# A linear-attention and token/channel mixer kernel: a corrected and searched plan, products of zeros ahead of the first work, transposes moved from TensorE to transfers

## The chip, the cores and the metric

The kernel runs on one NeuronCore of a Trainium2 chip. The core has five engines that run their own queues in order and meet at semaphores: TensorE (PE in the profile; its weight loads are shown apart as PEld), VectorE (DVE), ScalarE (ACT), GpSimd (POOL) and SyncE (SP), which here only issues transfers. The metric is the device time of one execution in microseconds.

## The reference, cut to what matters

Inputs: q, k, v, f_logit of shape (4 batches, 8 heads, 768 steps, 48), and four weight matrices. The output is (4, 768, 384).

```
f = 1 / (1 + exp(-f_logit))
for t in range(768):
    state = f[:, :, t, :, None] * state + outer(k[:, :, t], v[:, :, t])
    y[:, :, t] = q[:, :, t] @ state
x = y, heads side by side                       # (4, 768, 384)
h = relu(x.T @ w_tok1) @ w_tok2                 # 768 -> 256 -> 768 over the steps
u = x + h.T
out = u + relu(u @ w_ch1) @ w_ch2               # 384 -> 1536 -> 384 over the channels
```

## The kernel before, in words

**Attention.** The 768 steps of a batch are cut into 6 chunks of 128. For a chunk, ScalarE makes the log of the gates (exp, ln and a bf16 copy, `gates`, lines 324 to 326) and VectorE or GpSimd the rounding rest (329, 332). TensorE sums the logs along the chunk (`sums`, 350 to 353; the 128 x 1 products of 350 and 351 give the chunk's whole sum). ScalarE takes the exponentials `G`, `Gi` and `glast` (361, 363, 366). VectorE scales q and k to `qh` and `kh` (369, 371). TensorE turns both, four 128 x 128 blocks each (`turn`, 382), VectorE copies the eight blocks from PSUM to `qkT` (386). `scores` (396) are eight products of 48 rows, two at a time in the two halves of the array's rows; VectorE masks them to `AmT` (403). `parts` (419) are eight products kh.T @ v, 64 columns wide, in the two halves of the array's columns; VectorE adds them to the running `state` (426, 429, 431), and ScalarE or GpSimd writes the bf16 copy `state_bd`, head by head on the diagonal (a helper, lines 311 and 315). `outs` makes y from the state of the chunk before (448) and from `AmT` and v (455); two copies bring y to `x_bf` and `x_nat` (helper, 311 and 313).

**Mixer.** For a batch: `tok1` 12 products (480) and two ReLUs to `h1T` (484), `tok2` 12 products (492), `u` = x + h (496), its bf16 copy `u_bf` (311), 18 transposes `ut` (508) with their copies to `uT` (513), `ch1` 24 groups of three products (524) with a ReLU each to `zT` (534 on ScalarE, 536 on VectorE), `ch2` 6 groups of twelve (546) with the last addition (552) and a store from SP (555).

**What sets the order.** Nothing is scheduled at run time. Every step is an `Op` with the engines that may run it, a rank, what it needs and makes, and a cost (`Plan.cost`). `Plan.order` simulates the engines with these costs: again and again it takes the op that can start first, and among equals the one of lower rank. It chooses the engine, and the PSUM bank (8 of them) out of the same simulation. The functions are then called in the order of the planned starts, which gives each engine its queue. The ranks come from `due` and `ranks`.

**Transfers.** f of batch 0 comes chunk by chunk from SP, everything else from GpSimd's queue, which casts fp32 to bf16; `mark` (270) is a small write on GpSimd that holds back an f load of SP. q, k, v and f have three buffers each. SP also issues the 24 stores of the output (192 KB each).

Of the kernel before, what the change touches and what calls it, by code (L numbers as in the profile page):

```python
# [17 lines left out]
NBANK = 8  # L18
RING = 16384

# [19 lines left out]
class Plan:  # L40
# [58 lines left out]
    def order(self):  # L99
        for op in self.ops:  # L100
            first = op.before | ({op.behind} if op.behind else set())
            op.missing = len(first)
            for x in first:
                x.after.append(op)
        free = {e: 0.0 for e in (PE, ACT, DVE, POOL, SP)}
        ready = {e: [] for e in free}
        banks = [0.0] * NBANK
        wire = 0.0
        landed: list = []
        done = []  # L110

        def offer(op):
            t = max([x.end for x in op.before], default=0.0)
            if op.kind[0] == "load" and op.engines == (POOL,) and op.kind[3]:
# [3 lines left out]
                for at, rows in reversed(landed):  # L118
                    held += rows
                    if held > RING:  # L120
                        t = max(t, at)
                        break
            for e in op.engines:
                ready[e].append((t + (WAKE[e] if t else 0.0), op))

        for op in self.ops:
            if not op.missing:
                offer(op)
        while len(done) < len(self.ops):
            best = None  # L130
            for e, line in ready.items():
                for t, op in line:
                    if op.engine is not None:
                        continue
                    t = max(t, free[e])
                    if op.bank is not None and op.bank.at is None:
                        t = max(t, min(banks) + 55)
                    if best is None or (t, op.rank) < best[0]:
                        best = ((t, op.rank), e, op)
            (t, _), e, op = best  # L140
            ready[e] = [(a, o) for a, o in ready[e] if o is not op and o.engine is None]
            if op.bank is not None and op.bank.at is None:
                op.bank.at = min(range(NBANK), key=lambda j: banks[j])
                banks[op.bank.at] = math.inf
            own, till = self.cost(op, e)
            op.engine, op.start = e, t
            free[e] = t + own
            op.end = t + till
            if op.kind[0] == "load":
                size = op.kind[3]  # L150
                if size:
                    wire = max(wire, t + 1700) + size
                    op.end = wire + 1100
                if size and e == POOL:
                    landed.append((op.end, op.kind[2]))
            if op.bank is not None:
                op.bank.users -= 1
                if not op.bank.users:
                    banks[op.bank.at] = op.end
            done.append(op)  # L160
            for x in op.after:
                x.missing -= 1
                if not x.missing:
                    offer(x)
        return sorted(done, key=lambda o: o.start)
# [7 lines left out]
def kernel(  # L173
# [20 lines left out]
    NB = 3  # L194
# [23 lines left out]
    G = [st([128, H, D], BF16, f"G{i}") for i in range(2)]  # L218
    Gi = [st([128, H, D], BF16, f"Gi{i}") for i in range(2)]
    qh = [st([128, H, 64], BF16, f"qh{i}") for i in range(2)]  # L220
    kh = [st([128, H, 64], BF16, f"kh{i}") for i in range(2)]
    qkT = [st([128, 8, 128], BF16, f"qkT{i}") for i in range(2)]
    AmT = [st([128, 8, 128], BF16, f"AmT{i}") for i in range(2)]
    glast = [st([128, HP], FP32, f"glast{i}") for i in range(2)]
    state = st([128, HP, D], FP32, "state")
    tsum = st([128, HP, D], FP32, "tsum")
    state_bd = [st([128, HP, 2 * D], BF16, f"state_bd{i}") for i in range(2)]
# [5 lines left out]
    uT = st([128, 3, S], BF16, "uT")  # L233
# [3 lines left out]
    ones_bf = st([128, 1], BF16, "ones_bf")  # L237
    banks = [ps.tile([128, 512], FP32, tag=f"ps{i}", name=f"ps_{i}") for i in range(NBANK)]
# [7 lines left out]

    def load(what, b, c=None, engine=POOL):
        for n in what:
# [6 lines left out]
            add(engine, 0.0, lambda eng=eng, into=into, of=of: eng.dma_start(out=into, in_=of),  # L255
# [4 lines left out]
    def load_w(name, dst, src, size):  # L260
        add(POOL, 0.0,
# [3 lines left out]
    def once(engine, fn, make, own):  # L265
        add(engine, 0.0, fn, make=make, kind=("fix", own, own))

    def mark(b, c):

        add(POOL, 0.0, lambda: nc.gpsimd.memset(f_sb[b][0:1, 0:1, c, 0:1], 0.0), make=[("f", b, c)],  # L270
# [8 lines left out]
    once(POOL, lambda: make_upper_triangular(nc, tri_bf, val=1.0, diag=True), ["tri"], 550)  # L279
    once(POOL, lambda: make_identity(nc, ident), ["ident"], 550)  # L280
    once(DVE, lambda: nc.vector.memset(ones_bf, 1.0), ["ones"], 60)
    for i in range(2):
        for n, tl in (("L", Lhi[i]), ("L", Llo[i])):
            once(DVE, lambda tl=tl: nc.vector.memset(tl[:, :, :, D:64], 0.0), [("L", i, c) for c in range(NCH)], 400)
        for n, tl in (("qh", qh[i]), ("kh", kh[i])):
            once(DVE, lambda tl=tl: nc.vector.memset(tl[:, :, D:64], 0.0), [(n, i)], 120)
        once(DVE, lambda i=i: nc.vector.memset(state_bd[i], 0.0), [("sbd", i)], 220)
    for c in range(1, NCH):
        load("kq", 0, c)
# [26 lines left out]


# [17 lines left out]
    def attention(b, c, r):  # L335
        i, nb = c % 2, b % NB
# [43 lines left out]
        def turn(src, o):  # L380
            for hp in range(HP):
                nc.tensor.transpose(turned()[:, o + hp, :], blk(src)[:, hp, :], ident)  # L382
# [3 lines left out]
        add(DVE, r, lambda: nc.vector.tensor_copy(qkT[i], turned()), make=[("qkT", i)], bank=p_t,  # L386
            kind=("el", 1024, True, 2))
# [11 lines left out]
        add(PE, r, lambda: None, need=[("qkT", i)], bank=p_a[0], kind=("mm", 1))  # L399
        two = add(PE, r, scores, need=[("qkT", i)], bank=p_a[1], kind=("mm", 270))  # L400
# [9 lines left out]
        if not last:  # L410
            p_d = Bank()

            def dg():
                return banks[p_d.at][:, 0:HP * D].rearrange("p (hp e) -> p hp e", e=D)

            def parts():
                for h in range(H):
                    hp, par = h // 2, h % 2
                    nc.tensor.matmul(dg()[par * 64:par * 64 + 64, hp, :], lhsT=kh[i][:, h, :],  # L419
                                     rhs=v_sb[nb][:, h, c, :], start=True, stop=True)  # L420

            add(PE, r, parts, need=[("kh", i), vk], bank=p_d, kind=("mm", 210))
            gb = glast[i].unsqueeze(2).broadcast_to((128, HP, D))
            small = ("el", HP * D, True, 1)
            if c == 0:
                add(DVE, r, lambda: nc.vector.tensor_tensor(state, dg(), gb, ALU.mult),
                    need=[("glast", i)], make=["state"], bank=p_d, kind=small)
            else:
# [187 lines left out]
```

## Time and profile before

| | |
|---|---|
| median of 3 runs | 189.12 us (188.26 to 189.91) |
| the profiled execution | 188.64 us, of which its span is 186.8 us (1.84 us lie around the span) |
| TensorE busy | 172.5 us, 92% of the span, 1768 products |
| VectorE, ScalarE, GpSimd busy | 129.7, 126.9, 65.9 us |
| first product of TensorE | 6.08 us after the start of the span |
| first `ch1` product of batch 0 | 37.75 us |
| transfers | 19.95 MB; GpSimd's casting loads take 91.9% of the transfer time |

How to read it: a product's duration on TensorE includes its way through the array, and products overlap, so the pace is the distance between starts: a row "x8" of the timeline shows the start of the first and the time until the last has ended. The chain of waits follows what ended last back to the start, end to end, so there the lengths add up to the span. An engine's idle time matters only where something on that chain waits for it.

### The profile page before, as it was taken

How to read it: one execution, taken by the hardware profiler on the slowest of the kernel's cores; microseconds unless marked ns; L12 is line 12 of the kernel's file. 1: busy time of each engine (PE TensorE's matmuls, PEld its weight loads, DVE VectorE, ACT ScalarE, POOL GpSimd, SP SyncE). 2: the span in 40 equal slices, each digit the busy share in tenths (PEclk: the TensorE clock that was granted, in tenths of full speed). 3: DMA queues.
4: the chain of work that ended last, by engine and by line, in shares of the span. 5: the costliest groups of instructions: out<-in, count | busy, mean ns of one | idle time of the engine just before them, and what ended most of it. 6: DMA issues, size and time to landing. Idle time of an engine off the chain costs nothing.

```text
span 186.8 us, 4480 instructions
## 1 busy us (share of the span) xinstructions
PE 172.5 (92%) x1768; PEld 109.6 (59%) x1768; DVE 129.7 (69%) x295; ACT 126.9 (68%) x309; POOL 65.9 (35%) x78
## 2 busy tenths in 40 slices
PE   0589997799999999999999999999999999999992
PEld 0256664366667656676665665766666656656650
DVE  4387985749998999999988758977686638300222
ACT  4779963779983499999999935657875116698000
POOL 7999893275791444504621411011011000000000
PEclk9999999999999999999999999999999999999998
DMA  7999999999999999999992121011000121110222
GB/s 102 140 171 154 156 208 245 186 160 194 143 135 238 174 149 172 242 200 109 83 116 14 52 78 42 0 46 44 4 0 4 55 75 40 46 42 0 81 91 84
DMA packets 88437, 19.95 MB, mean 107 GB/s; under 512 B 81152, under 2 KB 87600, under 8 KB 88416
## 3 DMA queue, kind: packets, MB, share of 16 engines
q0 software_dynamic: 78720, 13.77, 91.9%
q1 hardware_dynamic: 9696, 5.90, 10.8%
q8 instruction: 14, 0.23, 0.5%
q14 instruction: 7, 0.06, 0.1%
HBM read 25.17 MB, written 4.72 MB: 160 GB/s over the span
## 4 chain that ended last, share of the span: by engine, by line
PE 84%; ACT 6%; DVE 3%; issue 2%; DMA 2%; POOL 1%; POOLq 0%; DVEq 0%; ACTq 0%
PE ps L524 26%; PE ps L546 24%; PE ps L382 7%; PE ps L480 5%; PE ps L396 4%; PE ps L492 3%; PE ps L455 3%; PE ps L419 3%; PE ps L352 2%; PE ps L508 2%; PE ps L353 2%; DMA f_sb<-in_f_logit_dram 2%; PE ps L448 2%; ACT u_bf L311 2%; ACT x_bf L311 1%
## 5 line engine op out<-in xcount | busy, mean ns | idle before, releaser
L546 PE MATMUL ps<-w_ch,zT 128*128 128x384 bf16 x288 | 54.1, 327 | 0.0
L524 PE MATMUL ps<-uT,w_ch 128*128 128x384 bf16 x288 | 52.6, 327 | 0.0
L534 ACT ACTIVATE zT<-ps 128x384 bf16<-128x384 f32 x76 | 36.5, 490 | 8.3 <-PE ps L524 7.9
L546 PEld LDWEIGHTS <-zT 128*128 128x128 bf16 x288 | 26.8, 98 | 16.5
L524 PEld LDWEIGHTS <-w_ch 128*128 128x128 bf16 x288 | 26.3, 97 | 15.9
L403 DVE TENSOR_TENSOR AmT<-ps,tri_bf 128x512 bf16<-128x512 f32 x48 | 30.6, 683 | 5.2 <-PE ps L396 5.0
L552 DVE TENSOR_TENSOR x_nat<-x_nat,ps 128x384 f32<-128x384 f32 x24 | 13.2, 550 | 22.9 <-PE ps L546 22.5
L255 POOL DMA_DIRECT2D q_sb<-in_q_dram x14 | 15.4, 1099 | 13.8 <-issue 5.7
L311 ACT ACTIVATE x_bf<-ps 128x384 bf16<-128x384 f32 x20 | 9.9, 494 | 12.9 <-PE ps L455 12.7
L255 POOL DMA_DIRECT2D k_sb<-in_k_dram x14 | 15.5, 1108 | 7.6 <-DMA f_sb<-in_f_logit_dram 4.5
L361 ACT ACTIVATE G<-ps 128x384 bf16<-128x384 f32 x24 | 11.7, 488 | 7.9 <-PE ps L353 7.8
L386 DVE COPY qkT<-ps 128x1024 bf16<-128x1024 bf16 x24 | 16.4, 685 | 0.8 <-PE ps L382 0.7
L255 POOL DMA_DIRECT2D v_sb<-in_v_dram x14 | 15.5, 1104 | 4.1 <-issue 2.5
L496 DVE TENSOR_TENSOR x_nat<-x_nat,ps 128x384 f32<-128x384 f32 x24 | 11.5, 548 | 4.1 <-PE ps L492 4.1
L311 ACT ACTIVATE u_bf<-x_nat 128x384 bf16<-128x384 f32 x24 | 11.4, 523 | 4.1 <-DVE x_nat L496 4.1
L315 POOL CAST state_bd<-state 48x192 bf16<-48x192 f32 x10 | 3.4, 343 | 29.8 <-DVE state L431 24.3
L324 ACT ACTIVATE f_sb<-f_sb 128x384 f32<-128x384 f32 x24 | 12.0, 523 | 2.7 <-DMA f_sb<-in_f_logit_dram 2.6
L480 PE MATMUL ps<-x_bf,w_tok 128*128 128x384 bf16 x48 | 12.3, 340 | 1.0 <-ACT x_bf L311 1.0
L536 DVE TENSOR_SCALAR zT<-ps 128x384 bf16<-128x384 f32 x20 | 10.4, 553 | 3.7 <-PE ps L524 3.6
L311 ACT ACTIVATE state_bd<-state 48x192 bf16<-48x192 f32 x30 | 10.8, 360 | 2.9 <-DVE state L431 2.6
L350 PE MATMUL ps<-ones_bf,Lhi 128*128 128x1 bf16 x80 | 7.0, 167 | 6.1 <-ACT Lhi L326 6.1
L326 ACT ACTIVATE Lhi<-f_sb 128x384 bf16<-128x384 f32 x24 | 12.2, 522 | 0.3
(58 smaller groups left out, 276.3 us busy)
## 6 DMA issues: line engine op xcount, KB each, us to landing
out_dram<-x_nat SPq DMA_DIRECT2D x24, 192.0 KB, 1.9
f_sb<-in_f_logit_dram POOLq DMA_DIRECT2D x3, 1152.0 KB, 11.0
f_sb<-in_f_logit_dram SPq DMA_DIRECT2D x6, 192.0 KB, 4.0
k_sb<-in_k_dram POOLq DMA_DIRECT2D x12, 96.0 KB, 6.3
q_sb<-in_q_dram POOLq DMA_DIRECT2D x12, 96.0 KB, 5.9
v_sb<-in_v_dram POOLq DMA_DIRECT2D x12, 96.0 KB, 6.0
w_ch<-in_moe_w_ch_dram POOLq DMA_DIRECT2D x2, 576.0 KB, 11.0
w_ch<-in_moe_w_ch_dram POOLq DMA_DIRECT2D x1, 1152.0 KB, 14.6
```

The lines of the kernel that those rows point to most:

```text
L255: add(engine, 0.0, lambda eng=eng, into=into, of=of: eng.dma_start(out=into, in_=of), make=[(n, b % NB, j) for j in (range(NCH) if c is No ...
L311: nc.scalar.activation(out_, in_, AF.Copy, bias=0.0, scale=1.0)
L324: add(ACT, r, lambda: nc.scalar.activation(fb, fb, AF.Exp, bias=0.0, scale=-1.0), make=[key], kind=el)
L326: add(ACT, r, lambda: nc.scalar.activation(hi, fb, AF.Copy, bias=0.0, scale=1.0), need=[key], make=[lk], kind=el)
L382: nc.tensor.transpose(turned()[:, o + hp, :], blk(src)[:, hp, :], ident)
L386: add(DVE, r, lambda: nc.vector.tensor_copy(qkT[i], turned()), make=[("qkT", i)], bank=p_t, kind=("el", 1024, True, 2))
L403: add(DVE, r, lambda p=p: nc.vector.tensor_tensor(AmT[i][:, 4 * p:4 * p + 4, :], banks[p_a[p].at].rearrange("s (hp t) -> s hp t", t=C), tb ...
L480: add(PE, rank("tok1", rt), lambda rt=rt, kt=kt, pm=pm: nc.tensor.matmul(banks[pm.at][:, 0:DM], lhsT=w_tok1[:, kt, rt * 128:(rt + 1) * 128 ...
L524: nc.tensor.matmul(banks[pm.at][:, 0:384], lhsT=w[:, kt, c0:c0 + 128], rhs=uT[:, kt, cols], start=(kt == 0), stop=(kt == 2))
L534: nc.scalar.activation(zT[:, cc, cols], banks[pm.at][:, 0:384], AF.Relu, bias=0.0, scale=1.0)
L546: nc.tensor.matmul(banks[pm.at][:, 0:DM], lhsT=zT[:, kt, tt * 128:(tt + 1) * 128], rhs=w_ch2[:, kt, :], start=(kt == 0), stop=(kt == 11))
L552: add(DVE, rank("ch2", tt), lambda un=un, pm=pm: nc.vector.tensor_tensor(un, un, banks[pm.at][:, 0:DM], ALU.add), make=[("x_nat", xn, tt)] ...
```

## The change

In the kernel it does eight things.

1. **The plan's model.** `Plan.order` is replaced by `attempt`, which simulates as before, with some mended costs: a product knows its way through the array ("row" for `scores`, "col" for `parts`, "" for the rest), a change of way takes `TURN` = 105 ns, and a ready product of another way is held back by rank (`HOLD`). Each engine starts at its own `FIRST`.
2. **The search.** `search` draws noise on the ranks, simulates again, and keeps what is no worse: 3000 tries on the part up to batch 0's `uT`, 800 on the whole. The seed is fixed, so the built order is always the same.
3. **Products of zeros.** Until 28.5 us of the plan's time the last PSUM bank is kept from other use, and wherever TensorE's plan has a hole a 128 x 128 product of zeros is put in (`rest`): 135 of them in the built program, 69 of these ahead of the first real product.
4. **Transposes by transfer.** In batches 2 and 3 (`TURNED`) `qh` and `kh`, now one tile `qkh`, are turned by one transposing transfer from SP into `qkT`, 12 in all, in place of 8 TensorE transposes and the VectorE copy. In batch 2 (`TURNED_U`) `u_bf` is turned by two such transfers. `uT` is laid out anew, [128, 6, 3, 128].
5. **Parts by pairs.** In batch 3 (not in `BYHEAD`) `parts` are four full products of 96 columns, of which the diagonal blocks are used, in place of eight narrow ones; the first VectorE step after them goes by halves of the partitions.
6. **Three buffers** in place of two for `G` to `state_bd` (`NI`).
7. **Freer engines.** The copies of y, and the ReLUs to `h1T`, may go to ScalarE or VectorE in every batch; in batch 0 the copy to `qkT` goes in two halves to either. `state_bd` is written by two full-height steps with a 0/1 scale (`own`), in batch 3 by ScalarE or GpSimd.
8. GpSimd makes the triangle and the identity in another order beside its loads.

In the order of the built program, counted: TensorE changes its way through the array 87 times before and 56 times after; from the first `ch1` product on 66 and 34 times. `turn` has 192 transposes before and 96 after, `ut` 72 and 54.

```diff
+TURN = 105
+HOLD = 2000.0
+WARM = 28500
+TRIES = (3000, 800)
+FIRST = {PE: 0.0, ACT: 0.0, DVE: 820.0, POOL: 1250.0, SP: 750.0}
...
+        if what == "turn":
+            return 1230, 2000 + 17 * n[0]
+        if what == "two":
+            return (470, 553) if engine == DVE else (514, 617) if engine == ACT else (700, 700)
...
+        free = dict(FIRST)
+        ready: dict = {e: {} for e in free}
+        banks = [0.0] * (NBANK - 1) + [WARM]
...
+                    if best is None or t <= best[0]:
+                        r = rank[k] + (HOLD if e == PE and self.ops[k].way not in (mode, None) else 0.0)
+                        if best is None or t < best[0] or r < best[1]:
+                            best = (t, r, e, k)
+            t, _, e, k = best
+            op = self.ops[k]
+            if e == PE and op.way is not None:
+                if op.way != mode:
+                    t = max(t, free[PE] + TURN)
+                mode = op.way
...
+            if op.kind[0] == "turn":
+                late = min(max(wire - t - 1000, 0), 2600)
+                wire = max(wire, t + 1500) + 16 * op.kind[1]
+                end[k] = t + till + late
...
+    def search(self, rank, tries, n, worth, rnd):
+        found = self.attempt(rank, n)
+        best, rank = worth(found), list(found[1])
+        for _ in range(tries):
+            far, share = rnd.choice((300, 1000, 3000)), rnd.choice((0.02, 0.1, 0.5))
+            other = [r + (rnd.gauss(0, far) if rnd.random() < share else 0) for r in rank]
+            now = self.attempt(other, n)
+            if worth(now) <= best:
+                best, rank = worth(now), other
+        return rank
...
+        head = self.search(rank[:n], TRIES[0], n, begin, rnd)
+        found = self.attempt(head + rank[n:])
+        rank = self.search(head + found[1][n:], TRIES[1], None, lambda found: found[0], rnd)
...
+        out, t = [], 1600.0
+        for o in sorted(self.ops, key=lambda o: o.start):
+            if o.engine == PE and o.kind[1] > 1:
+                while t < min(o.start, WARM) - 250:
+                    out.append((t, rest))
+                    t += 56 if t > 4500 else 107
+                t = max(t, o.start + self.cost(o, PE)[0])
+            out.append((o.start, o.fn))
...
-    NB = 3
+    NB, NI = 3, 3
+    SPLIT = (0,)
+
+    TURNED_U, TURNED = (2,), (2, 3)
+    BYHEAD = (0, 1, 2)
...
-        add(PE, r, lambda: turn(qh[i], 0), need=["ident", ("qh", i)], bank=p_t, kind=mms(*[C] * 4))
-        add(PE, r, lambda: turn(kh[i], 4), need=["ident", ("kh", i)], bank=p_t, kind=mms(*[C] * 4))
-        add(DVE, r, lambda: nc.vector.tensor_copy(qkT[i], turned()), make=[("qkT", i)], bank=p_t,
-            kind=("el", 1024, True, 2))
+        if b in TURNED:
+            add(SP, r, lambda: nc.sync.dma_start_transpose(qkT[i], qkh[i].rearrange("t n d -> t (n d)")),
+                need=[("qh", i), ("kh", i)], make=[("qkT", i, 0), ("qkT", i, 4)], kind=("turn", 64))
+        else:
+            add(PE, r, lambda: turn(blk(qh[i]), 0), need=["ident", ("qh", i)], bank=p_t, kind=mms(*[C] * 4))
+            add(PE, r, lambda: turn(blk(kh[i]), 4), need=["ident", ("kh", i)], bank=p_t, kind=mms(*[C] * 4))
...
+                dg2 = banks[p_d.at][:, 0:DM].rearrange("p (h e) -> p h e", e=D)
+                for hp in range(HP):
+                    nc.tensor.matmul(dg2[:, 2 * hp:2 * hp + 2, :], lhsT=blk(kh[i])[:, hp, :],
+                                     rhs=v_sb[nb][:, 2 * hp:2 * hp + 2, c, :], start=True, stop=True)
...
+            op = add(ACT if b <= 2 else (ACT, POOL), r, None, need=["own", ("state", 0), ("state", D)], make=[("sbd", i)], kind=("two",))
+
+            def spread(op=op):
+                for par in range(2):
+                    half = state_bd[i][:, :, par * D:par * D + D]
+                    if op.engine == ACT:
+                        nc.scalar.activation(half, state, AF.Copy, bias=0.0, scale=own[:, par:par + 1])
+                    else:
+                        nc.gpsimd.tensor_scalar(half, state, own[:, par:par + 1], None, ALU.mult)
...
-            op = add(ACT if b == 0 else (ACT, DVE), r, None, make=[key], bank=p_y, kind=el)
+            op = add((ACT, DVE), r, None, make=[key], bank=p_y, kind=el)
...
+        if b in TURNED_U:
+            for th in range(2):
+                tts = slice(3 * th, 3 * th + 3)
+                add(SP, rank("ut", 3 * th), lambda tts=tts: nc.sync.dma_start_transpose(
+                    uT[:, tts].rearrange("p tt d t -> p (tt d) t"), u_bf[:, tts, :].rearrange("t tt d -> t (tt d)")),
+                    need=[("u_bf", tt) for tt in range(3 * th, 3 * th + 3)],
+                    make=[("uT", d, tt) for tt in range(3 * th, 3 * th + 3) for d in range(3)], kind=("turn", 72))
...
+    def rest():
+        nc.tensor.matmul(banks[NBANK - 1][:, 0:128], lhsT=nil, rhs=nil, start=True, stop=True)
+
+    nc.vector.memset(nil, 0.0)
+    for fn in plan.order(rest):
+        fn()
```

More of the change, by code (lines that the diff above doesn't have):

```diff
@@ L97, in cost, with attempt, offer @@
         return n[0], n[1]
[L99 to L108, printed above, removed]
+    def attempt(self, rank, n=None):
+        n = n or len(self.ops)
+        missing = [len(o.first) for o in self.ops[:n]]
+        start, end, engine, at = [0.0] * n, [0.0] * n, [None] * n, {}
+        users = {b: b.users for b in self.banks}
+        free = dict(FIRST)
+        ready: dict = {e: {} for e in free}
+        banks = [0.0] * (NBANK - 1) + [WARM]
+        wire, mode = 0.0, ""
         landed: list = []
-        done = []
-        def offer(op):
-            t = max([x.end for x in op.before], default=0.0)
+        left = n
+        def offer(k):
+            op = self.ops[k]
+            t = max([end[x] for x in op.data], default=0.0)
             if op.kind[0] == "load" and op.engines == (POOL,) and op.kind[3]:
@@ L117, in offer @@
                 held = op.kind[2]
-                for at, rows in reversed(landed):
+                for when, rows in reversed(landed):
                     held += rows
                     if held > RING:
-                        t = max(t, at)
+                        t = max(t, when)
                         break
             for e in op.engines:
[L124 to L128, printed above, removed]
@@ L129, in order @@
-        while len(done) < len(self.ops):
-            best = None
-            for e, line in ready.items():
[L132 to L144, printed above, removed]
+                ready[e][k] = t + (WAKE[e] if t else 0.0)
@@ L145, in order @@
             own, till = self.cost(op, e)
-            op.engine, op.start = e, t
+            engine[k], start[k] = e, t
             free[e] = t + own
[L148 to L155, printed above, removed]
+            end[k] = t + till
@@ new lines, in attempt @@
+        return max(end), start, end, engine, at
+    def search(self, rank, tries, n, worth, rnd):
[8 more added lines that the diff above has]
+        return rank
@@ L433, in attention @@
-            for rows, cols in ((slice(0, D), slice(0, D)), (slice(64, 64 + D), slice(D, 2 * D))):
-                op = add(ACT if b <= 2 else POOL, r, None, need=["state"], make=[("sbd", i, cols.start)],
-                         kind=("el", HP * D, False, 1))
-                op.fn = lambda op=op, rows=rows, cols=cols: copy_on(
-                    op.engine, state_bd[i][rows, :, cols], state[rows])
+            whole, halves = (slice(0, 128), None, (0, D)), []
+            for rows, cols in ((slice(0, 64), slice(0, D)), (slice(64, 128), slice(D, 2 * D))):
+                halves.append((rows, cols, (cols.start,)))
```

209 lines of the change are left out of this document (144 added, 65 removed).

## The prediction, made before the changed kernel had run

> **What bounds the kernel now.** I read the page first: busy time, the slices, and the chain that ended last.
>
> ```profile
> PE 172.5 (92%) x1768; PEld 109.6 (59%) x1768; DVE 129.7 (69%) x295; ACT 126.9 (68%) x309; POOL 65.9 (35%) x78
> ...
> PE   0589997799999999999999999999999999999992
> ...
> PE 84%; ACT 6%; DVE 3%; issue 2%; DMA 2%; POOL 1%; POOLq 0%; DVEq 0%; ACTq 0%
> ```
>
> 84% of the chain is TensorE. The digits below 9 lie in the first eight slices (37 us) and the last. Next the waits of TensorE, in total:
>
> ```profile
> PE ps L350 <- ACT Lhi L326: 6.1, 1, 6.1
> PE ps L480 <- ACT x_bf L311: 1.0, 2, 0.6
> PE ps L396 <- DVE qkT L386: 0.8, 1, 0.8
> ```
>
> Apart from the first 6.1 us no wait totals over 1.0 us. Then TensorE's timeline, for its pace.
>
> ```profile
> 26.04 1.06 PE L382 MATMUL ps<-ident,kh 128*128 128x128 bf16 x8
> 26.89 1.17 PE L480 MATMUL ps<-x_bf,w_tok 128*128 128x384 bf16 x3
> ...
> 33.12 2.33 PE L492 MATMUL ps<-h1T,w_tok 128*128 128x384 bf16 x12 [0.41 <-ACT h1T L484]
> ...
> 37.75 6.50 PE L524 MATMUL ps<-uT,w_ch 128*128 128x384 bf16 x39
> ...
> 54.56 0.81 PE L546 MATMUL ps<-w_ch,zT 128*128 128x384 bf16 x4
> 55.30 0.40 PE L396 MATMUL ps<-qkT 48*128 48x128 bf16 x8
> 55.63 0.82 PE L546 MATMUL ps<-w_ch,zT 128*128 128x384 bf16 x4
> ...
> 171.40 11.86 PE L546 MATMUL ps<-w_ch,zT 128*128 128x384 bf16 x72
> ```
>
> Eight transposes take 26.89 - 26.04 = 0.85 us early, 106 ns each; four at 53.15 take 0.23, 56 each. Until 28.5 us every product runs at half pace, though the slices' granted clock reads 9 there. The last 72 products, chain time 11.71 us, give 162 ns for 384 columns. The two groups around 55.30 price a change of the array's way: four products should take 0.65 but the scores start after 0.74. The chain shows both exits:
>
> ```profile
> 46.95 0.24 PE ps L419 x8
> 47.19 0.59 PE ps L524 x3
> ...
> 54.72 0.65 PE ps L546 x4
> 55.37 0.33 PE ps L396 x8
> 55.70 0.76 PE ps L546 x4
> ```
>
> 0.76 against 0.65 for four, 0.59 against 0.49 for three: 0.10 us per change, in or out. Scores cost (0.33 - 0.10)/8 = 29 ns each, parts (0.24 - 0.09)/8 = 19.
>
> **A check by adding up.** From the first ch1 at 37.75 us to the end TensorE has 576 ch and 72 tok products x 162 ns = 105.0; 144 + 54 transposes x 56 = 11.1; sums 36 x 162 and 120 x 25 = 8.8; scores 144 x 29 = 4.2; parts 120 x 19 = 2.3; y 60 x 42.5 and 144 x 25 = 6.2; 66 changes x 0.10 = 6.6. Sum 144.2. The trace has 145.3 (37.75 to 183.1, the last start plus its 0.16), so real stalls are 1.1 us, and 3.7 us follow (the last addition, a store of 1.9, the end). This part is TensorE's queue; before it lies a stretch bound by waits, half pace and loads.
>
> **Part by part.**
>
> *Transfers in place of transposes.* 96 x 56 = 5.4 us for q and k, 18 x 56 = 1.0 for u leave TensorE, all in the dense part. VectorE loses 12 copies of 685 ns and 6 of 348, 10.3 us beside the path. It is needed: VectorE is busy 19.1 and 18.9 of 20 us from 60 to 100 us, and a denser TensorE asks the rest of its work sooner.
>
> The cost is the wait. `scores` now wait for a transfer, and behind them in TensorE's queue stands everything else. In the built order I added up TensorE's work between a chunk's `sums` and its `scores`: batch 2 11.2, 17.8, 16.4, 15.5, 23.3, 27.0 us; batch 3 7.0, 11.5, 10.9, 17.7, 10.0, 7.8. Before, batch 3 had 4.3 to 6.1 and no stall. Of the 4.3, 0.45 + 0.2 went to the transposes and 0.7 to the copy, so exponentials and scaling need at most 2.9. That leaves 4.1 and 4.9 us for the two tightest transfers, 7 or more for the others. For u, 6.25 us lie between the third tok2 and ch1; addition and cast took at most 2.2 before, so 4.05 are left (about 0.4 less where GpSimd casts: its nearest row, L332, has 933 ns against 523). ScalarE's queue loses nothing by that.
>
> No transposing transfer is in the trace. SP's stores bound it: 1.9 us for 192 KB in the median, 7.0 at worst, between 56 and 85 us under the loads. A q, k transfer has 256 KB, so 2.5 at the quiet rate. I take 3, by the quiet row, since the tight ones lie after the last load landed (99 us); 2.5 and 7.0 stay as ends. [...] SP's stores stand behind waiting transfers; their tiles are three deep, so this is free. VectorE must wait for a transfer before it rewrites `qkh` three chunks later, with masks and ReLUs queued behind; at 3 us that is covered by the same slack. I enter 1.3 us of new stalls, between 0 and the 7.0 end's sum (2.9 + 2.1 + 3.0 = 8).
>
> *Order.* 66 changes become 34: -3.2 us, paid by holding scores and parts back, which the slack above already contains.
>
> *Pairs.* 40 x 19 = 0.8 becomes 20 x 42.5 = 0.85; the gain is in the changes counted. Five more VectorE halves of about 0.35 are beside the path.
>
> *New uT layout.* ch1 now reads three runs of 128. `sums` reads eight runs of 48 and keeps 161 ns, so nothing. Three transposes of batch 0 fall behind its first ch1: +0.2.
>
> The dense part: 144.2 - 5.4 - 1.0 - 3.2 + 0.2 = 134.8.
>
> *Zeros and the start.* 135 products have no waits; in a hole they cost nothing, ahead of ready work at most 0.06 to 0.11 each. The first stand where TensorE waits until 6.08. If they hold full pace, the chain's half-pace pieces between 8.98 and 30.4 us, about 13 us of TensorE, halve; then others are late. Bound below: chunk 5's q is issued at 16.53 and lands by the median of 5.9 at 22.4; scaling 0.7, turning 0.6, half copy 0.4, scores 0.55, four masks of two chunks 2.4, y 0.4, copy 0.5, tok1 0.5, ReLU 0.55 end at 29.0; ch1 followed that ReLU (33.45) by 4.3: 33.3. Bound above: 37.75, no gain. VectorE is the tightest engine there: its operations in the new order up to that ch1, by the rows' durations, sum to 29.0 us, less 0.08 for each of 51 overlaps (two masks take 1.28, not 1.37), is 25 from 6.06: 31 without idling. It idled 7.8 before; I leave it half: 35.0, a gain of 2.75.
>
> [...]
>
> *The rest* (three buffers, freer engines, `state_bd` at full height, masks made in another order) changes no TensorE product and no row by more than 0.1; I enter nothing, and its cover is the other engines' idle, 57 us of VectorE's span.
>
> Sum: 35.0 + 134.8 + 1.1 + 1.3 + 3.7 = 175.9 of span, against 186.8. With the 1.84 around it 177.7, against 188.64. The median lies 0.5 above that execution: 178.2.
>
> **The rivals.**
>
> *Transfers land late: slower.* If they take L us, stalls sum to (L - 4.1) + (L - 4.9) + (L - 7.1) and, for u, (L - 4.05), each where positive. It takes 12.2 us to lose the gain: L = 8.1. At 10 us they are 5.9 + 5.1 + 2.9 + 6.0 = 19.9, and two of 1.5 to 2 beside: 200. For it: stores of 7.0 us exist, and the software loads are 91.9% of the transfer time. Against: those were under loads, and batch 3's fall after them.
>
> [...]
>
> *ScalarE or VectorE become the bound.* From 60 to 100 us they are busy 36.1 and 37.9 of 40. TensorE wants that work in about 10% less time; where batch 1's share (no transfers there) can't follow, 4 us come back: 182. Against: TensorE was stalled for 0.5 us there, and batch 2's copies leave.
>
> **How the numbers follow.** Forecast 0.62 (its own range 175 to 180.5: the start's 33.3 and 37, stalls of 0 to 3), half pace 0.14, other engines 0.13, late transfers with 8.1 us or more 0.07, something unseen 0.04, half of it slower. The range 174.5 to 184 takes in the first three, and two of these together in part. About 1% (1.9 us) can be told from no change. Faster by over 1% means under 187.2: 0.62 + 0.14 + 0.12 + 0.01 = 0.89; slower by over 1%: 0.05 + 0.02 = 0.07; within 0.04.
>
> **What would show it.** Right: 128-column starts 56 ns apart from about 6 us; the first ch1 of batch 0 at 33 to 37; from there about 135 us of TensorE with waits under 3 us in total; transposing transfers landing in 2.5 to 4 us. Wrong: a wait of `scores` or ch1 for a transfer near the top of TensorE's waits, starts of 107 ns after 8 us, or masks and ReLUs in VectorE's queue as its releasers between 60 and 100 us.

## The result, and the profile after

The changed kernel takes 186.63 us in the median of four runs (185.97 to 186.88), the kernel before 188.69 in the four runs beside it: a ratio on record of 0.9875 [0.9827, 0.9922] (the two medians alone give 0.989). It is a little over 1% faster, 8.4 us short of the 178.2 forecast and outside the range of 174.5 to 184. The profiled execution took 186.78 us, of which the span is 185.0. Medians here and below are over all executions; the ratios leave out the slow ones, one each of x_late (its profiled one, whose span is therefore not used), x_nozero and y_byhead.

The new code has other line numbers: `scores` is L504, `parts` L528, the turn on TensorE L483, the turning transfer L486, `outs` L582 and L589, `ut` L648, `ch1` L665, `ch2` L682, the scaling of q and k 470 and 472, the masks 513, the zeros 721. First the page of the changed kernel, its busy times, slices and chain:

```profile
span 185.0 us, 4485 instructions
...
PE 168.1 (91%) x1769; PEld 108.8 (59%) x1769; DVE 128.8 (70%) x301; ACT 123.2 (67%) x303; POOL 67.8 (37%) x75
...
PE   7977887798999999875997999999999999999992
...
PEclk9999999999999999997899999999999999999999
...
PE 48%; DMA 31%; POOL 13%; issue 6%; DVE 0%; POOLq 0%
```

Where 84% of the chain was TensorE, 31% of it is now transfers; by line the page gives 14% to `w_ch`'s load, 9 to the turning transfers and 8 to v's load. The PE row has a dip that it did not have, the 8, 7 and 5 of the seventeenth to nineteenth slice, 74 to 88 us at 4.6 us a slice, and a 7 at 97 to 102; the clock row dips at 83 to 92. The waits of TensorE in the changed kernel:

```profile
PE ps L504 <- DMA qkT<-qkh: 4.2, 2, 3.2
PE ps L483 <- DVE qkh L470: 1.6, 3, 0.8
PE ps L648 <- ACT u_bf L406: 1.2, 4, 0.5
PE ps L528 <- DMA v_sb<-in_v_dram: 1.1, 2, 0.6
```

The first is the one that the prediction named as the sign of being wrong. The second lies between 10 and 19 us, in batch 0, ahead of the first `ch1`; most of the third and half of the fourth come ahead of it too. TensorE's timeline shows where it stands; in brackets is the idle time before a row and what ended it.

```profile
81.28 1.01 PE L648 MATMUL ps<-ident,u_bf 128*128 128x128 bf16 x9 [0.18 <-ACT u_bf L406]
85.53 0.57 PE L504 MATMUL ps<-qkT 48*128 48x128 bf16 x8 [3.24 <-DMA qkT<-qkh]
...
99.54 0.40 PE L504 MATMUL ps<-qkT 48*128 48x128 bf16 x8 [0.99 <-DMA qkT<-qkh]
```

And the chain of waits over the same stretch (start, length, what):

```profile
68.48 7.89 DMA v_sb<-in_v_dram
76.36 9.12 DMA qkT<-qkh
...
85.53 0.57 PE ps L504 x8
86.10 0.43 PE ps L648 x3
86.53 1.92 PE ps L665 x6
88.45 0.64 PE ps L648 x6
89.09 2.92 PE ps L665 x18
92.01 7.49 DMA qkT<-qkh
```

The transfer of batch 2's first chunk is issued at 76.36 us and takes 9.12, where 3 had been entered. (The chain names v's load as what released it, but v landed at 78.21, after the issue; VectorE's scaling of k, 75.95 to 76.30, is what it had to wait for.) After the stand six `ch1` products take 1.92 us, 320 ns each, before eighteen take 2.92, 162 each: the pace had halved. That costs 0.95 us on `ch1`, 0.31 and 0.16 on the transposes and 0.24 on the scores (against 56 ns, 0.10 for the change of way and 0.33), 1.7 in all. The granted clock reads 0.50 between 85.6 and 89.0 us.

**The prediction's sum, set against the traces.** Every span is split as the prediction split it: first `ch1` of batch 0, TensorE's work from there by the predicted prices and the counts of the built program, the part after the last product's start, and what is left, called stall.

| kernel | median us | ratio to before | span | first ch1 | work | stall | end |
|---|---|---|---|---|---|---|---|
| before | 188.69 | 1 | 186.8 | 37.75 | 144.1 | 1.1 | 3.9 |
| as predicted | 178.2 | | 175.9 | 35.0 | 134.8 | 2.4 | 3.7 |
| after | 186.63 | 0.9875 [0.9827, 0.9922] | 185.0 | 36.20 | 134.8 | 10.1 | 3.9 |

Of the 9.1 us between 175.9 and 185.0, 1.2 are in the start, 7.7 in stalls and 0.2 at the end (the way of counting: the prediction had the last product's own 0.16 us in the work). The work left TensorE as counted; stalls took its place, 5.6 of the 10.1 us between 80 and 90 us, 1.6 in the ten before 100, 1.3 in those before 80 and 0.9 in the forties.

### The profile page after: what moved, and what is told of

It reads as the page before. It is cut to its first block, busy times and chain, and to the rows that moved or that the text cites. A ratio compares the mean times of both kernels' runs of the same rounds, so it can differ in the third digit from the quotient of the medians.

```text
span 185.0 us, 4485 instructions
## 1 busy us (share of the span) xinstructions
PE 168.1 (91%) x1769; PEld 108.8 (59%) x1769; DVE 128.8 (70%) x301; ACT 123.2 (67%) x303; POOL 67.8 (37%) x75
## 3 DMA queue, kind: packets, MB, share of 16 engines
q1 hardware_dynamic: 24736, 9.64, 24.4%
## 4 chain that ended last, share of the span: by engine, by line
PE 48%; DMA 31%; POOL 13%; issue 6%; DVE 0%; POOLq 0%
PE ps L682 19%; PE ps L665 17%; DMA w_ch<-in_moe_w_ch_dram 14%; DMA qkT<-qkh 9%; DMA v_sb<-in_v_dram 8%; POOL q_sb L344 4%; POOL k_sb L344 4%; POOL v_sb L344 2%; PE ps L614 2%; PE ps L625 2%; PE ps L504 2%; POOL f_sb L344 1%; PE ps L589 1%; PE ps L648 1%; PE ps L582 1%
## 5 line engine op out<-in xcount | busy, mean ns | idle before, releaser
L682 PE MATMUL ps<-w_ch,zT 128*128 128x384 bf16 x288 | 54.0, 326 | 0.0
L665 PE MATMUL ps<-uT,w_ch 128*128 128x384 bf16 x288 | 51.1, 330 | 0.8 <-DVE uT L653 0.8
L665 PEld LDWEIGHTS <-w_ch 128*128 128x128 bf16 x288 | 27.8, 99 | 18.5 <-DVE uT L653 0.9
L414 ACT ACTIVATE zT<-ps 128x384 bf16<-128x384 f32 x67 | 31.8, 491 | 7.3 <-PE ps L665 6.8
L682 PEld LDWEIGHTS <-zT 128*128 128x128 bf16 x288 | 26.8, 98 | 16.3
L416 DVE TENSOR_SCALAR zT<-ps 128x384 bf16<-128x384 f32 x29 | 15.0, 553 | 7.5 <-PE ps L665 7.3
L344 POOL DMA_DIRECT2D q_sb<-in_q_dram x14 | 15.4, 1097 | 13.4 <-issue 10.2
L567 ACT ACTIVATE state_bd<-state,own 128x192 bf16<-128x192 f32 x36 | 14.4, 450 | 5.1 <-DVE state L559 4.3
L406 ACT ACTIVATE x_nat<-ps 128x384 f32<-128x384 f32 x14 | 6.9, 491 | 10.5 <-DVE x_bf L408 8.4
L425 ACT ACTIVATE f_sb<-f_sb 128x384 f32<-128x384 f32 x24 | 11.8, 517 | 2.9 <-DMA f_sb<-in_f_logit_dram 2.6
L504 PE MATMUL ps<-qkT 48*128 48x128 bf16 x192 | 9.0, 221 | 5.0 <-DMA qkT<-qkh 4.2
L464 ACT ACTIVATE Gi<-ps 128x384 bf16<-128x384 f32 x24 | 11.8, 497 | 2.5 <-DVE AmT L513 1.2
L629 DVE TENSOR_TENSOR x_nat<-x_nat,ps 128x384 f32<-128x384 f32 x24 | 11.5, 549 | 1.8 <-PE ps L625 1.8
L426 ACT ACTIVATE f_sb<-f_sb 128x384 f32<-128x384 f32 x24 | 12.0, 517 | 0.1
L430 DVE TENSOR_TENSOR Llo<-f_sb,Lhi 128x384 bf16<-128x384 f32 x18 | 9.7, 552 | 3.1 <-ACT Lhi L427 3.1
```

What stands on the lines that cost most here:

```text
L344: add(engine, turn_of(), lambda eng=eng, into=into, of=of: eng.dma_start(out=into, in_=of), make=[(n, b % NB, j) for j in (range(NCH) if c ...
L414: nc.scalar.activation(out_, in_, AF.Relu, bias=0.0, scale=1.0)
L416: nc.vector.tensor_scalar(out_, in_, 0.0, None, ALU.max)
L426: add(ACT, r, lambda: nc.scalar.activation(fb, fb, AF.Ln, bias=1.0, scale=1.0), make=[key], kind=el)
L504: nc.tensor.matmul(banks[p_a[par].at][:, hp * 128:(hp + 1) * 128], lhsT=qkT[i][rows, 4 + hp, :], rhs=qkT[i][rows, hp, :], start=True, stop ...
L567: nc.scalar.activation(half, state, AF.Copy, bias=0.0, scale=own[:, par:par + 1])
```

## The experiments

Theory A: batch 2's transfers share the transfer engines with batch 3's loads of f, k, q and v, are late by that, and TensorE stands. Rivals: B, VectorE is full between 60 and 100 us and delays what TensorE asks for; C, the plan prices a transfer too low, so a search with the right price would hide it. For the start: zeros against order. The recorded expectations use the letters more loosely: C is also q of batch 2 landing late with VectorE's queue behind it (x_noload3) and the rewriting of `qkh` (x_late), and B is also a stall by the order itself (x_noturn). Where that matters the text says which is meant.

Each ratio is to the kernel before, in runs on the same chip beside it. Where an edit changes the plan, the search draws another order; how much that alone moves is the subject of one run.

**Batch 3's loads left out (x_noload3).** The order is unchanged; batch 3 works on what batch 0 left in the buffers.

```diff
-  lambda ...: eng.dma_start(out=into, in_=of)
+  lambda ...: None if b == 3 else eng.dma_start(out=into, in_=of)
```

> The changed kernel in the same order on every engine, but the four loads of batch 3 (f, k, q, v, planned between 73 and 95 us) are left out, so batch 3 works on what batch 0 left in the buffers. Theory A (batch 2's transposing transfers are late because batch 3's loads fill the transfer engines): transfers issued from 76 us land in 3 to 4.5 us instead of 7.5 to 9.9, TensorE's wait of 4.2 us for them goes below 1 us, and the span falls from 185.0 to 176 to 180 us. Rival B (VectorE and ScalarE are the bound there, 19.5 of 20 us busy): TensorE still loses 6 us or more between 75 and 100 us, the span stays over 183. Rival C (the first transfer is late because q of batch 2 lands at 73 and VectorE queues before it): about half, 180 to 183, with one wait of 1 to 2 us left at 78 to 82 us.

183.04 us, ratio 0.971 [0.9646, 0.9773]; the stall falls from 10.1 to 5.1. The transfer's line in the changed kernel (durations of the issue on SP, min/median/max, then issue to landing):

```profile
L486 SPq DMA_TRANSPOSE qkT<-qkh x12: 1232/1252/4257, 76.4 to 140.6; - x12
...
DMA to landing us min/median/max: 3.0/4.3/9.9
```

The same line without batch 3's loads:

```profile
L486 SPq DMA_TRANSPOSE qkT<-qkh x12: 1232/1247/2115, 76.7 to 136.0; - x12
...
DMA to landing us min/median/max: 3.0/3.1/4.8
```

The same program, with the loads and without: 9.1, 9.9, 8.1 and 7.5 us for batch 2's first four transfers become 4.1, 3.2, 3.1 and 3.0. TensorE's wait for them is gone, and so is the half pace. Theory A holds for the mechanism: in these two executions it is worth 5.0 of the 10.1 us; by the medians it is 3.6. The amount is smaller than theory A expected: the span of 180.4 lies just outside its 176 to 180, and in the range that the expectation gave to its rival C, though that rival's wait of 1 to 2 us at 78 to 82 us is not there (0.34 and 0.30).

**Batch 2's q and k turned on TensorE again (x_turn3).**

```diff
-    TURNED_U, TURNED = (2,), (2, 3)
+    TURNED_U, TURNED = (2,), (3,)
```

> Batch 2's q and k are turned on TensorE again, with VectorE's copies; batch 3's and batch 2's u stay with transfers. The plan is searched anew. TensorE has 3.0 us more work than in the changed kernel (48 transposes and 3 changes of way). Theory A: the 8 us that TensorE lost between 75 and 100 us shrink to 2 or less, so about 185.0 - 8 + 2 + 3.0 = 180 to 182 of span. Rival B: VectorE gets 4.1 us of copies back in its fullest stretch, and the span is 185 or more.

183.94 us, ratio 0.9764 [0.9712, 0.9816]. Work rises by 2.9 to 137.7 us, stall falls by 6.2 to 3.9. In this order, doing less of the change gives more: it is faster than the changed kernel, and their intervals don't overlap (a second seed below weakens that). The span of 182.2 is just outside theory A's 180 to 182.

**No transfers at all (x_noturn).** `TURNED_U, TURNED = (), ()`.

> No transposing transfer at all, in any batch; the mended plan, the search, the zeros, the pairs and the buffers stay. TensorE has 7.4 us more work than in the changed kernel (96 + 18 transposes and 10 more changes of way). If the transfers are the whole trouble, TensorE loses about 1 to 2 us after its first ch1 as before the change, and the span is 36.2 + 142.2 + 1.5 + 3.7 = 183 to 185: the transfers gained and lost about the same. If the order itself stalls TensorE (rival B), 187 or more.

190.17 us, ratio 1.0092 [1.0055, 1.0129]: slower than before. The rest of the change takes 1.4 us from the start (36.37) and 1.9 from the work (142.2), but stalls rise from 1.1 to 5.7. The span of 188.2 lies in the expectation's last range, 187 or more, where the order itself stalls TensorE. So in these two orders the transfers carry the gain, late as some of them are.

**The plan's price of a late transfer raised (x_late).** In the plan a queued transfer adds at most 2.6 us.

```diff
-                late = min(max(wire - t - 1000, 0), 2600)
+                late = min(max(wire - t - 1000, 0), 6500)
```

> Only the price in the plan: a transposing transfer beside loads may be planned up to 6.5 us later instead of 2.6. Same instructions, another order. Theory A: scores of batch 2 are queued later, TensorE's wait for transfers falls from 4.2 to under 2 us, span 178 to 182. Rival C: VectorE still waits for the transfers before it rewrites the scaled q and k, so the wait moves to the masks and the span stays at 183 or more.

186.27 us, ratio 0.9858 [0.9772, 0.9943], no different from the changed kernel. TensorE no longer waits for a transfer, but batch 2's then take 8.8 to 11.3 us, and VectorE waits 2.6 us for two of them before it rewrites `qkh`. That is what the expectation called rival C there: the wait moves to VectorE. The idea that the right price in the plan would hide the wait is not borne out in this one order; another seed or more tries were not run.

**The zeros left out, order unchanged (x_nozero).**

```diff
-                    out.append((t, rest))
```

> The changed kernel in the same order without the 135 products of zeros (the last PSUM bank still kept back). If they hold TensorE's clock: without them 128-column products start 106 ns apart until 25 us or later as before the change, and the first ch1 of batch 0, at 36.2 us with them, comes at 37.5 to 38.5; the span grows by 1 to 2 us from 185.0. Rival: TensorE's pace is not what bounds the start (loads and VectorE are), then the first ch1 stays within 0.4 us of 36.2 and the zeros bought nothing.

187.37 us, ratio 0.9899 [0.9855, 0.9942]. TensorE's timeline without the zeros:

```profile
23.55 0.63 PE L482 MATMUL ps<-ident,qkh 128*128 128x128 bf16 x4
24.11 0.41 PE L527 MATMUL ps<-v_sb,qkh 128*64 128x48 bf16 x8
24.46 0.40 PE L482 MATMUL ps<-ident,qkh 128*128 128x128 bf16 x4
24.69 0.33 PE L581 MATMUL ps<-state_bd,qkT 128*128 128x96 bf16 x4
...
36.43 3.74 PE L664 MATMUL ps<-uT,w_ch 128*128 128x384 bf16 x22
```

Four transposes before 24.11 take 0.56 us, 115 ns each less the change of way; those from 24.46 take 0.23, 57 each. So the pace was half until about 24.4 us, and yet the first `ch1` is at 36.43, against 36.20 with the zeros. In the changed kernel, with the zeros, the full pace does come early:

```profile
0.98 5.30 PE L721 MATMUL ps<-nil 128*128 128x128 bf16 x69 [0.98 <-DVE nil L723]
...
36.20 6.01 PE L665 MATMUL ps<-uT,w_ch 128*128 128x384 bf16 x36
```

69 in 5.30 us are 77 ns each, the first 2.7 us of them at 107 and the rest at 56. Full pace twenty microseconds earlier moves the first `ch1` by 0.2 us, and even that can't be told from nothing: x_noload3, z_mask and z_noload3_mask run the same order up to there, zeros included, and have it at 36.58, 37.31 and 37.29. The rival's condition, within 0.4 us, is met and 37.5 is not reached; a gain well under 1 us would stay unseen in this spread. So no run shows TensorE's pace to be what bound the start.

The zeros also have a cost that was not counted. Without them the first sum of logs starts as soon as its input is there:

```profile
5.71 0.19 PE L450 MATMUL ps<-ones_bf,Lhi 128*128 128x1 bf16 x1 [5.71 <-ACT Lhi L426]
```

and the second, which needs VectorE's rest, at 6.30. With them it stands behind all 69, and how long these take depends on when the pace doubles: 2.7 us after the first zero in the changed kernel, where the 69 take 5.30 us; in z_noload3_mask they take 6.70, which puts it at about 5.6, an estimate by the same 107 and 56 ns. In x_noload3:

```profile
0.98 6.43 PE L721 MATMUL ps<-nil 128*128 128x128 bf16 x69 [0.98 <-DVE nil L723]
7.25 0.17 PE L451 MATMUL ps<-ones_bf,Lhi 128*128 128x1 bf16 x1
```

So the zeros held the first real work back by about 1 us there, and by nothing in the changed kernel's trace, where it starts at 6.12. Fewer zeros were not tried.

**No search (x_nosearch).** `TRIES = (0, 0)`.

> The changed kernel with the mended plan as it comes from the ranks, without the random search (0 tries in both parts). If the search shortens the start, the first ch1 comes at 37 us or later; if it also spaces the work, the stall after it (10.1 us in the changed kernel) is larger, and the span is 188 or more. Rival: the search fits the order to a model that is wrong where it stalls, and is worth under 1 us either way: 184 to 186.

192.78 us, ratio 1.0188 [1.0143, 1.0234]; first `ch1` 39.54, stall 11.7. The mended model with its first order alone is slower than the kernel before by 1.9%; this draw of the search is worth 6 us to it. Part of that is the clock again: around three waits for transfers (0.95, 2.25 and 0.82 us) it reads 0.50 from 87.6 to 97.7 us (0.973 in the mean over the span).

**Variants of x_turn3.** First, two of batch 2's transfers kept, those of chunks 4 and 5, which come after batch 3's loads (y_c45):

```diff
-        if b in TURNED:
+        if b in TURNED or b == 2 and c >= 4:
```

> As x_turn3 (span 182.2), but chunks 4 and 5 of batch 2, whose scaling comes when the loads are ending, are turned by transfer too: TensorE's work falls by 1.0 us. Theory A: these two transfers land in 3 to 5 us and the span is 181 to 182. If they still meet the loads (7 us and more), the gain is lost: 182.5 or more.

183.79 us, ratio 0.9723 [0.9682, 0.9764], the lowest median of the kernels that leave no work out, not told apart from x_turn3. The two land in 4.7 and 3.0 us; TensorE waits 0.2 us for them.

Batch 3's u by transfer too (y_u23): `TURNED_U, TURNED = (2, 3), (3,)`.

> As x_turn3 (span 182.2), but batch 3's u is turned by two transfers as well. TensorE's work falls by 1.4 us (18 transposes, 4 changes of way). No load runs then, so the transfers land in 3 us; TensorE has ch2 of batch 2 to do meanwhile. If that covers them, 180.5 to 181.5; if not, a wait of ch1 for the transfer of 1 us or more shows and the span is 182 or more.

186.38 us, ratio 0.9856 [0.9823, 0.9889]; work 136.4, stall 8.7. The waits of TensorE in it begin with

```profile
PE ps L665 <- DMA uT<-u_bf: 1.7, 2, 1.4
```

Some of it is the transfer, 1.4 us in one wait as the expectation's second case had it; more is other waits of another order.

Holding back by rank switched off (y_hold0): `HOLD = 0.0`.

> x_turn3 (span 182.2, 37 changes of way and 3.9 us of stall after the first ch1) with HOLD at 0: the plan still prices a change of way but no longer holds a ready product back, 71 changes in all instead of 59. If the stall that is left between 60 and 100 us comes from masks asked for in bursts, it falls to 1 to 2 us and pays for the 1.2 us of changes: 181 to 182.5. If VectorE and ScalarE are simply full there, the stall stays near 4 us and the span grows to 183 to 184.

186.64 us, ratio 0.9866 [0.9823, 0.9909]; work rises to 139.1 by the changes of way, stall is 4.7 against 3.9. In this order holding products back is not what makes the stalls.

Batch 3's `parts` by heads again (y_byhead): `BYHEAD = (0, 1, 2, 3)`.

> x_turn3 with batch 3's parts by heads again (no pairs): 12 more changes of way, 1.2 us more, less 0.05 for the narrower products. If the pairs are worth what the count says, the span is 183 to 184; if VectorE's five extra halves had cost as much, it stays at 182.

188.56 us, ratio 0.9956 [0.9924, 0.9989]: work 139.0, as counted 1.3 more, but stall 6.5. More than the edit explains, so I asked how much an order by itself moves. Another seed, `random.Random(2)` for `random.Random(1)`, of x_turn3 (y_seed2) and of y_c45 (y_c45s2):

> x_turn3 with another seed of the search, nothing else. It says how far the time of a newly searched plan moves by the draw alone. I expect 181 to 184 of span: within 1% of x_turn3's time; if it lies 2 us or more away, a single searched kernel does not show an edit worth less than that.

> y_c45 with another seed. y_c45 had 136.8 us of work, 3.5 of stall, but its first ch1 only at 37.96; with the first ch1 at 36.2 as in x_turn3 the span would be 180.2. I expect 180 to 183.

185.58 us (ratio 0.9828 [0.9787, 0.9869]) for 183.94, and 185.40 (0.981 [0.9772, 0.9849]) for 183.79. The seed alone moves the ratio by 0.7 and 0.9%, so one re-planned kernel tells nothing of an edit worth under 2 us, y_u23, y_hold0 and y_byhead among them. That x_turn3 and y_c45 beat the changed kernel rests on stalls of 3.5 to 5.8 in four orders against 10.1; the size, 1.0 to 2.8 us, depends on the seed. With the second seed x_turn3's interval overlaps the changed kernel's, and the changed kernel itself was run with one seed only.

**Is VectorE the bound?** 5.1 us of stall remain without the loads. The windows of the changed kernel and of x_noload3 (busy of 20 us: PE, PEld, DVE, ACT, POOL; then clock, transfer share, GB/s), the changed one first, from 60 to 80 us:

```profile
60.00:80.00 20.00, 19.14 (x249) 12.68 (x246) 19.49 (x46) 18.41 (x50) 8.13 (x4) 1.00 2.03 183
```

Without batch 3's loads:

```profile
60.00:80.00 20.00, 19.39 (x251) 12.85 (x248) 19.49 (x45) 18.03 (x49) 4.42 (x2) 1.00 2.01 163
80.00:100.00 20.00, 18.68 (x188) 11.47 (x187) 19.60 (x48) 18.66 (x49) 5.51 (x6) 1.00 0.31 63
```

VectorE is at 19.5 of 20 us, which looks like rival B. To test it, the masks of batches 1 and 2 were cut to 64 of 512 columns, in an unchanged order; the rest of these masked scores stays what the buffer held.

```diff
-                AmT[i][:, 4 * p:4 * p + 4, :],
...
+            w = 16 if b in (1, 2) else C
...
+                AmT[i][:, 4 * p:4 * p + 4, 0:w],
```

On x_noload3 (z_noload3_mask):

> x_noload3 (span 180.4, 5.1 us of stall, 3.6 of it between 70 and 100 us) in the same order, and in batches 1 and 2 the masks on VectorE write 64 columns of 512 (the rest of the masked scores is left as it was). VectorE has 24 x 0.45 = 11 us less to do between 40 and 100 us. If VectorE's fullness is the rest of the stall (rival B's share), the 3.6 us fall below 1 and the span is 177 to 178.5; if they come from the order or from waits for loads, they stay and the span is 180 or more.

182.40 us, ratio 0.9667 [0.9591, 0.9743]. Its window from 60 to 80 us:

```profile
60.00:80.00 20.00, 18.64 (x266) 12.75 (x263) 15.19 (x44) 17.63 (x49) 4.43 (x2) 1.00 2.05 175
```

VectorE has 4.8 us to spare between 60 and 80, and 2.2 in the next 20, and the stall is 4.8, after 5.1. On the changed kernel itself (z_mask) and on x_turn3 (z_turn3_mask):

> The changed kernel in the same order with its loads, and the same narrow masks in batches 1 and 2. If VectorE's fullness makes the first transfer late (issued at 76.4 us), it goes out earlier and the span falls by 3 us or more, to 182 or less; if the loads alone do it (q of batch 2 lands at 73, v at 78, transfers take 8 to 10 us whenever they start), the transfers still take 7.5 us or more, TensorE still waits 3 us or more for them, and the span is 182.5 to 184.5.

> x_turn3 (span 182.2, 3.9 us of stall) in the same order with the narrow masks in batches 1 and 2. If VectorE is what is left, the stall falls to 1.5 us or less and the span to 179.5 to 180.5; else 181.5 or more.

z_mask: 185.33 us, ratio 0.9824 [0.9754, 0.9893], not told apart from the changed kernel; batch 2's first four transfers still take 7.9, 8.7, 6.9 and 7.4 us, two of them a little under the 7.5 expected, and the first is issued no earlier, at 77.28. The stall is 7.0, TensorE's waits for transfers 1.8 instead of 4.2, where 3 or more had been expected: in that execution the first `ch1` was 1.1 us later (37.31) and the first transfer landed at 85.2 as before, so TensorE came later to the same wait, stood 1.34 us instead of 3.24, and went on at full pace (six `ch1` products in 0.98 us). z_turn3_mask: 184.74 us, ratio 0.9778 [0.9708, 0.9847], stall 3.5 after 3.9. Rival B falls: with a fifth of VectorE free, the transfers are issued as late and the rest of the stall stays. What z_mask shows in its place is ScalarE: ahead of the scaling in VectorE's queue stands a copy of y that is released by ScalarE's own copy of it, and VectorE, with time to spare, stood idle 2.05 us for that until 75.66 us. From 66 to 76 us ScalarE was busy 10.00 of 10 us there, and 9.99 in the changed kernel. That is read from the traces; no run lightens ScalarE.

What remains, 3 to 5 us, has no single place. In x_noload3 the profile names 2.5 of the 5.1 us, in six waits: batch 0's last `uT` at 43.5 (0.75 us), `zT` at 93.9 (0.43), the masks at 95.5 and 73.2 (0.37 and 0.27), batch 2's v at 78.4 (0.34) and `u_bf` at 81.7 (0.30); the rest is in shorter gaps. The waits for scaled q and k on L483 are not part of it: they lie in batch 0, before the first `ch1`. None of this was tried by an experiment: earlier loads for batch 2, or a freer ScalarE (18 to 19 of 20 us), stay open.

## Why the prediction was wrong

- **What leaves TensorE: right.** Transfers 6.4, changes of way 3.2, the rest 0.2 back: the changed kernel's count, at the predicted prices, gives the 134.8 forecast. What the timeline has over these prices is the stall, most of it in the eighties, where the transfers were late.
- **The price of a transfer: the step that failed.** "I take 3, by the quiet row, since the tight ones lie after the last load landed (99 us)" was true of batch 3, whose transfers landed in 3.0 to 4.9 us with no wait, and of u, 2.8 to 3.0. It was used for batch 2 as well, whose first four were issued at 76.4 to 92.0 us, under batch 3's loads. There the row for stores, 7.0 at worst, was the near one, and 9.9 was reached. In the prediction's sum this is the term of 1.3 us of new stalls: with the 1.1 carried over it made 2.4, and 10.1 came. x_noload3 shows 5.0 of the 7.7 us between them to be the late transfers and what they set off.
- **Batch 2's slack: sized too large.** 11.2 us between sums and scores less 2.9 for scaling were to leave 8.3. In the trace the chunk's sums ended at 69.1 us and its q landed only at 72.97; VectorE then had masks and a copy ahead of it, and the scaling was done at 76.3, 7.2 us after the sums, where 2.9 had been entered. TensorE was ready for the scores at 82.3, so 5.9 us were left. A quiet transfer would have fitted even then; the 9.12 us one was 3.2 late.
- **The cost of a stand: left out.** After 3.24 us idle the pace was half until 89 us, 1.7 us more. And the wait on VectorE that was called covered, the rewriting of `qkh`, was 2.6 us.
- **The start: half the size, and not seen to come from the pace.** "About 13 us halve; then others are late" was to give 2.75 us; 1.55 came. VectorE's part of the estimate was near: from 6.06 us to the first `ch1` it is busy 25.5 us where 25 were counted, and idle 4.7 where 3.9 were left (7.4 before, by the same windows). But x_nozero has the first `ch1` within the spread of the executions that have the zeros, so no gain from the pace is shown; and "ahead of ready work at most 0.06 to 0.11 each" left out that the 69 stand there together, about 1 us in x_noload3. What gives the 1.55, the new order or the freer engines, was not taken apart, except that without the search the first `ch1` is 3.3 us later.
- **The rivals.** Late transfers were right in kind, with "against: those were under loads, and batch 3's fall after them" the sentence that put them aside for the wrong batch. Half pace in the start, given 0.14, was gone in the changed kernel (starts 56 ns apart from 3.7 us on), and without the zeros it was not seen to be the bound. VectorE as the bound was worth 0.3 and 0.4 us of stall where masks were narrowed and no transfer was late; ScalarE, the other half of that rival, was full ahead of batch 2's first transfer and was not tried.
- **What stays open.** x_noturn's stall of 5.7 us and x_noload3's of 5.1 say that even without a late transfer the 2.4 entered was too little. The order before stood at 1.1 in the same work; fewer changes of way and a searched order did not keep that, and why is not shown.

## What to carry to other kernels

A transfer that takes the place of work on an engine has the price of the moment at which it is issued (here 3.0 us in a quiet stretch, up to 9.9 under loads): look up what else is on the transfer engines there, chunk by chunk, and take the row measured under that load. Move only the pieces that fall in a quiet stretch; in the orders drawn here half the change was better than the whole. Before work is put in ahead of the real work to bring an engine's full pace early (here at 3.7 us instead of about 24.4), check that the engine's pace is what the first results wait for. Before judging an edit to a kernel whose order is searched, run the same kernel with another seed, and for a cause use an edit that leaves the order as it is.

## What the runs showed of the hardware

- A transposing transfer of 256 KB took 3.0 to 3.1 us quiet, and one of u's, 288 KB, 2.8 to 3.0. The plain store of 192 KB takes 1.9 in the median; scaled by size, an estimate, that is 2.5 and 2.85. In quiet the transposing transfers of u took about that, those of q and k a fifth more. Beside GpSimd's casting loads the first four of q and k took 7.5 to 9.9 us. Their issue held SP for 1.23 us, and up to 4.26 then.
- The loads were slower too: batch 3's k took 15.7 us to land where it had taken 10.7, its q 16.3 for 8.7. In the issue rows of the changed kernel (KB each, median us to landing, here over batches 2 and 3), where 11.5 and 9.2 stood before, and 10.7 and 9.8 in x_turn3, which turns batch 2's q and k on TensorE:

```profile
k_sb<-in_k_dram POOLq DMA_DIRECT2D x2, 576.0 KB, 14.5
q_sb<-in_q_dram POOLq DMA_DIRECT2D x2, 576.0 KB, 12.8
```

- With products of zeros first, the distance between their starts fell from 107 to 56 ns 2.7 us after the first in the changed kernel, at 3.7 us of the span, and after about 5.6 in z_noload3_mask, by the estimate above; without them the pace was half until about 24.4 us (x_nozero). At the start of the span the clock row reads 9 all the while (granted clock 1.00 from 0 to 4 us), so the pace has to be read from the starts.
- After a stand of 3.24 us the pace was half for 3.4 us in the changed kernel; in x_nosearch, around waits for transfers of 0.95, 2.25 and 0.82 us, it was half for 10.2 us (granted clock 0.50 from 87.6 to 97.7 us).
